# Windowed attention and a gated feed-forward in one kernel: the later attention blocks taken two at a time

## The chip, the core and the metric

The kernel runs on one core of one Trainium2 chip. The metric is the device time of one execution in microseconds (us). Before the change the median of three runs is 900.22 us (897.39, 900.22 and 904.76). The profiled execution of the same kernel took 901.14 us, of which 899.3 us lie between its first and its last instruction (the span).

## The reference

```python
scores = scale * q @ k.T                       # 8 batches, 8 heads, 576 positions, 64 wide
rel = pos[:, None] - pos[None, :]
mask_plain = (rel >= 0) & (rel < 32)                         # heads 0 to 3
mask_dil = (rel >= 0) & (rel < 128) & (rel % 4 == 0)         # heads 4 to 7
attn = softmax(where(mask, scores, -1e9))
x = (attn @ v), heads side by side             # 4608 rows of 512
h = x @ w_in                                   # 512 to 2048
g = h * clip(h + 3, 0, 6) / 6
out = g @ w_out                                # 2048 to 512
```

All of it is float32.

## The kernel before, in words

The **attention** is cut into 48 pieces `t`, called trios here. Since a query sees 32 keys at most (in the dilated heads too, once the host has sorted positions by their residue), a trio is 24 small problems: 32 queries against 64 keys. `block(ts, tv)` puts two trios on TensorE together: the scores of trio `ts` (`mm_scores`, L193, 24 products with a 64x32 weight) and, between them, the values of an earlier trio `tv` (`mm_values`, L211, 24 products). Each of these float32 products shows as two loads and two matmuls in the trace, so such a block is 96 loads and 96 matmuls. Its two results stand in two PSUM buffers.

Behind a block, for the scores: VectorE adds the mask (L222), takes the largest of each row (L226, `largest`) and subtracts it (L230, `shifted`), ScalarE takes the exponential (L239). The result `e` is turned by `turn_by_blocks`: two transposes on VectorE (L326, L327) and four DMAs of 24 KB on SyncE's queue (L330), which gives `a`, the weights of the value products. For the values: VectorE divides by the sums (L244, L245, L247, `normalise`), gives `x`, and the same `turn_by_blocks` makes `xf` of it. `st_split` then cuts `xf` in a high part `xh` (ScalarE, L358) and a low part `xl` (GpSimd, L363), the operands of the feed-forward. `shifted` also issues the load of a later trio's queries and keys (`kq`, 416 KB) and `normalise` that of a later trio's values (`v`, 390 KB), both on SyncE's queue; the pool `loads` has `NLOAD` = 3 buffers of each.

The **feed-forward** goes through 12 chunks of 384 rows and, for each chunk, 16 slices of the 2048 middle columns: one step `n` for each. A step is `gemm1(n)` on TensorE (12 matmuls of 384 columns, L458 to L460, into one of the two PSUM buffers of the pool `ps_h`), then `relu` on ScalarE (L466), `gate` on VectorE (L469, which sets the `ps_h` buffer free), `gate_high` on ScalarE (L473), `gate_low` on VectorE (L477), and two steps later `gemm2` on TensorE (9 matmuls of 512 columns, L490 to L492), which adds to three PSUM buffers of the pool `ps_a`. That pool has six buffers; three hold a chunk's sums, the others serve the attention. So a step is 21 matmuls and 21 weight loads. The tiles `e`, `a`, `x`, `xf`, `t`, `gh`, `gl` come from one pool `work` of `WORK` = 12 buffers.

The trios 0 to 11 and the first two chunks are worked off by a list written out by hand (`ORDER`). From trio 12 on, trios are set between the feed-forward steps by the table `at` near the end: `halves` counts half steps from the first step of chunk 2 (place 2s stands between `gemm1` and `gemm2` of step s, place 2s + 1 behind its `gemm2`). `st_both(t + 1, t)` at place `at[i]` makes one block (scores of trio t + 1, values of trio t) and its VectorE and ScalarE work; `xf` is turned one place later, `a` two places later, `st_split` four places later. There are 37 such blocks: the first with scores alone, 35 with both, the last with values alone. They stand 6 or 7 places apart at first and then 8, that is four steps. TensorE's order is the program's own; the other engines' order is made by a scheduler at build time, from priorities. A chunk's first `gemm1` waits for the `xl` of the last trio that has rows in it: in the steady part, one chunk in three has its last trio only six places ahead.

## Time and profile before

| what | before |
| --- | --- |
| median of three runs | 900.22 us |
| profiled execution | 901.14 us |
| its span | 899.3 us |
| TensorE matmuls (PE) | 884.3 us busy, 98% of the span, 8732 |
| TensorE weight loads (PEld) | 790.0 us busy, 8732 |
| VectorE (DVE) | 448.7 us busy, 50% |
| ScalarE (ACT) | 345.7 us busy, 38% |
| GpSimd (POOL) | 43.7 us busy, 5% |
| granted TensorE clock, mean | 0.99 |
| first changed block | at 176 us of the span |

PE in these rows is TensorE's matmuls, PEld its weight loads, which run beside them; SPq is SyncE's queue, on which most DMAs are issued. A matmul's duration is modelled and overlaps that of the next, so the distance from one start to the next says what one costs. "idle before <-" names what ended an engine's idle time; "issue" is idle time that ends with nothing that the profile shows. Where a group of rows has "waits", it is put down to the producer that came last.

### The profile page before, as it was taken

The numbers are of one execution on the slowest core, as the hardware profiler recorded it, in microseconds if no ns is written. First come the engines' busy times: TensorE is split into PE (matmuls) and PEld (weight loads), VectorE is DVE, ScalarE is ACT, GpSimd is POOL, SyncE is SP. The second block draws the span as 40 slices with busy tenths as digits, with TensorE's granted clock in tenths as the row PEclk, the third lists the DMA queues.
The fourth block names the chain that finished last, engine by engine and source line by source line (L and its number), as shares of the span: only waits on it lengthen the run. The fifth ranks groups of instructions, "written<-read, shape, count | busy, mean of one in ns | idle before, by whom it ended". The sixth has DMA issues, their size and how long they took to land.

```text
span 899.3 us, 20600 instructions
## 1 busy us (share of the span) xinstructions
PE 884.3 (98%) x8732; PEld 790.0 (88%) x8732; DVE 448.7 (50%) x951; ACT 345.7 (38%) x661; POOL 43.7 (5%) x60
## 2 busy tenths in 40 slices
PE   7899999999999999999999999999999999999998
PEld 4688898889898989998999899889988898899997
DVE  4799997245455545444444444454445444422221
ACT  3688775333333333323333333223333333322322
POOL 0000000000110100000010001000100000000000
PEclk8799999999999999999999999999999999999999
DMA  8746435122232213113212222122113210100000
GB/s 280 265 147 209 121 115 200 56 86 89 65 112 79 62 56 114 51 48 101 70 51 82 70 65 86 47 82 88 51 46 99 71 33 11 47 3 1 36 1 35
DMA packets 37803, 74.87 MB, mean 83 GB/s; under 512 B 7376, under 2 KB 16592, under 8 KB 37712
## 3 DMA queue, kind: packets, MB, share of 16 engines
q1 hardware_dynamic: 32528, 64.13, 23.3%
q10 hardware_dynamic: 5184, 9.44, 2.8%
q8 instruction: 68, 1.11, 0.5%
q14 instruction: 23, 0.19, 0.1%
HBM read 57.02 MB, written 9.44 MB: 74 GB/s over the span
## 4 chain that ended last, share of the span: by engine, by line
PE 95%; DVE 1%; ACT 1%; DMA 1%; SPq 1%; issue 1%; DVEq 0%; ACTq 0%
PE ps_o L490 15%; PE ps_h L458 15%; PE ps_h L460 14%; PE ps_h L459 14%; PE ps_o L492 14%; PE ps_o L491 14%; PE ps_a L211 3%; PE ps_a L193 2%; PE ps_a L203 1%; PE ps_a L296 1%; SPq L330 1%; DMA mi<-in_mask 0%; DMA a<-a_t 0%; PE ps_a L270 0%; DVE x L247 0%
## 5 line engine op out<-in xcount | busy, mean ns | idle before, releaser
L458 PE MATMUL ps_h<-xh,wt 128*128 128x384 f32 x768 | 261.0, 340 | 0.0
L469 DVE SCALAR_TENSOR_TENSOR t<-t,ps_h 128x384 f32<-128x384 f32 x192 | 106.3, 553 | 306.5 <-ACT t L466 306.2
L460 PE MATMUL ps_h<-xh,wt 128*128 128x384 f32 x768 | 258.7, 337 | 0.0
L459 PE MATMUL ps_h<-xl,wt 128*128 128x384 f32 x768 | 258.6, 337 | 0.0
L490 PE MATMUL ps_o<-wt,gh 128*128 128x512 f32 x576 | 228.2, 396 | 0.0
L492 PE MATMUL ps_o<-wt,gl 128*128 128x512 f32 x576 | 224.6, 390 | 0.0
L491 PE MATMUL ps_o<-wt,gh 128*128 128x512 f32 x576 | 224.2, 389 | 0.0
L466 ACT ACTIVATE t<-ps_h,three 128x384 f32<-128x384 f32 x192 | 111.0, 579 | 267.5 <-PE ps_h L460 260.0
L477 DVE TENSOR_TENSOR gl<-t,gh 128x384 fp32r<-128x384 f32 x192 | 107.1, 558 | 100.7 <-ACT gh L473 99.1
L458 PEld LDWEIGHTS ps_h<-xh,wt 128*128 128x128 f32 x768 | 144.9, 189 | 7.4
L459 PEld LDWEIGHTS ps_h<-xl,wt 128*128 128x128 f32 x768 | 144.8, 189 | 6.7
L460 PEld LDWEIGHTS ps_h<-xh,wt 128*128 128x128 f32 x768 | 144.8, 189 | 0.0
L473 ACT CAST gh<-t 128x384 fp32r<-128x384 f32 x192 | 98.4, 513 | 101.3 <-DVE t L469 96.7
L492 PEld LDWEIGHTS ps_o<-wt,gl 128*128 128x128 f32 x576 | 108.1, 188 | 23.4
L490 PEld LDWEIGHTS ps_o<-wt,gh 128*128 128x128 f32 x576 | 108.1, 188 | 18.7 <-issue 0.3
L491 PEld LDWEIGHTS ps_o<-wt,gh 128*128 128x128 f32 x576 | 108.2, 188 | 15.8
L363 POOL TENSOR_TENSOR xl<-xf,xh 128x384 fp32r<-128x384 f32 (+3 forms) x54 | 43.1, 808 | 740.6 <-ACT xh L358 675.4
L239 ACT ACTIVATE e<-e 128x384 f32<-128x384 f32 x48 | 25.1, 524 | 112.1 <-DVE e L230 112.1
L358 ACT CAST xh<-xf 128x384 fp32r<-128x384 f32 (+3 forms) x72 | 33.7, 536 | 37.0 <-DMA xf<-xf_t 36.8
L193 PE MATMUL ps_a<-kq 64*32 64x64 f32 x1872 | 46.6, 225 | 0.0
L211 PEld LDWEIGHTS ps_a<-v,a 64*32 64x32 f32 x1728 | 36.0, 105 | 10.7 <-issue 9.2
L211 PE MATMUL ps_a<-v,a 64*32 64x65 f32 x1728 | 42.4, 225 | 0.6 <-DMA a<-a_t 0.6
(46 smaller groups left out, 495.0 us busy)
## 6 DMA issues: line engine op xcount, KB each, us to landing
st<-in_w SPq DMA_DIRECT2D x32, 512.0 KB, 4.1
kq<-in_qk SPq DMA_DIRECT2D x39, 416.0 KB, 4.5
v<-in_v SPq DMA_DIRECT2D x39, 390.0 KB, 3.7
out<-o ACTq DMA_DIRECT2D x36, 256.0 KB, 2.9
first<-in_qk SPq DMA_DIRECT2D x9, 416.0 KB, 5.1
first<-in_v SPq DMA_DIRECT2D x9, 390.0 KB, 5.8
a<-a_t SPq DMA_DIRECT2D x144, 24.0 KB, 1.8
xf<-xf_t SPq DMA_DIRECT2D x144, 24.0 KB, 1.8
```

What stands on the lines that cost most here:

```text
L193: return nc.tensor.matmul(ps[at : at + QB, 2 * QB * i : 2 * QB * (i + 1)], lhsT=x[rows, KW + QB * n : KW + QB * (n + 1)], rhs=x[rows, QB * ...
L211: return nc.tensor.matmul(ps[at : at + QB, i * W : (i + 1) * W], lhsT=ats[t][rows, QB * n : QB * (n + 1)], rhs=vs[t][rows, n, :], start=Tr ...
L458: nc.tensor.matmul(ph, lhsT=wt[f][:, 0, ks], rhs=a, start=(kt == 0), stop=False)
L459: nc.tensor.matmul(ph, lhsT=wt[f][:, 0, ks], rhs=b, start=False, stop=False)
L460: ins = nc.tensor.matmul(ph, lhsT=wt[f][:, 1, ks], rhs=a, start=False, stop=(kt == NK - 1))
L466: return nc.scalar.activation(ts[n], phs[n], AF.Relu, bias=three, scale=1.0)
L469: return nc.vector.scalar_tensor_tensor(out=ts[n], in0=ts[n], scalar=6.0, in1=phs.pop(n), op0=ALU.min, op1=ALU.mult)
L473: return nc.scalar.copy(ghs[n], ts[n])
L477: return nc.vector.tensor_tensor(out=gls[n], in0=ts.pop(n), in1=ghs[n].bitcast(F32), op=ALU.subtract)
L490: nc.tensor.matmul(po[c][tt], lhsT=gh[:, rows], rhs=wt[f][:, 2], start=first, stop=False)
L491: nc.tensor.matmul(po[c][tt], lhsT=gh[:, rows], rhs=wt[f][:, 3], start=False, stop=False)
L492: ins = nc.tensor.matmul(po[c][tt], lhsT=gl[:, rows], rhs=wt[f][:, 2], start=False, stop=(f == NF - 1))
```

## The change

`st_both` becomes `st_pairs(ts, tv)`: two blocks directly behind each other, scores of ts and ts + 1 and values of tv and tv + 1. Four results need four PSUM buffers at once: the first block's scores stand in a buffer of the pool `ps_h` (the first product's), the other three in `ps_a`. The table `at` now holds one place for two trios: 1, 13, 25, 41, 57 and then every 16 places, eight steps; all of them are odd, behind a `gemm2`. Both `xf` are turned at the pair's own place, both `a` one place later, and `st_split` follows four and five places later. There are 19 such groups: one of two scores-only blocks, 17 pairs with both, one of two values-only blocks. `NLOAD` goes from 3 to 2 (so `ORDER` no longer loads `k14` and `v14`), `WORK` from 12 to 16. The lines behind `st_pairs` move by 10: L330 is now L340, L458 to L460 are L468 to L470, and so on.

```diff
-WORK = 12
+WORK = 16
-NLOAD = 3
+NLOAD = 2
...
-... k12 k13 k14 v12 v13 v14 M2 ...
+... k12 k13 v12 v13 M2 ...
...
-    def block(ts, tv):
+    def block(ts, tv, pool=ps_a, tag="ps_a"):
-        ps = ps_a.tile([P, 512], F32, name="ps_a") if ts is not None else None
+        ps = pool.tile([P, 512], F32, name="ps_a", tag=tag) if ts is not None else None
...
-    def st_both(ts, tv):
-        block(ts, tv)
-        if tv is not None:
-            normalise(tv)
-        if ts is not None:
-            largest(ts)
-            shifted(ts)
-            exponent(ts)
+    def st_pairs(ts, tv):
+        for i in range(2):
+            first = dict(pool=ps_h, tag="ps_h") if i == 0 else {}
+            block(ts and ts + i, tv and tv + i, **first)
+        if ts is not None:
+            largest(ts)
+        if tv is not None:
+            normalise(tv)
+        if ts is not None:
+            largest(ts + 1)
+        if tv is not None:
+            normalise(tv + 1)
+        if ts is not None:
+            for t in (ts, ts + 1):
+                shifted(t)
+                exponent(t)
...
-    at = [1 + 19 * i // 3 for i in range(10)]
-    at += [at[-1] + 8 * (i + 1) for i in range(T - NFIRST - 10)]
+    at = [1, 13, 25, 41, 57]
+    at += [at[-1] + 16 * (i + 1) for i in range((T - NFIRST) // 2 - len(at))]
-    place(-3, lambda: st_both(NFIRST, None))
-    place(-1, lambda: ats.update({NFIRST: turn_by_blocks(es.pop(NFIRST), "a")}))
+    place(-3, lambda: st_pairs(NFIRST, None))
+    place(-3, lambda: ats.update({t: turn_by_blocks(es.pop(t), "a") for t in (NFIRST, NFIRST + 1)}))
     for i, p in enumerate(at):
-        t = NFIRST + i
-        more = t + 1 < T
-        place(p, lambda t=t, more=more: st_both(t + 1 if more else None, t))
-        place(p + 1, lambda t=t: xfs.update({t: turn_by_blocks(xs.pop(t), "xf")}))
-        if more:
-            place(p + 2, lambda t=t: ats.update({t + 1: turn_by_blocks(es.pop(t + 1), "a")}))
-        place(p + 4, lambda t=t: st_split(t))
+        t = NFIRST + 2 * i
+        more = t + 2 < T
+        place(p, lambda t=t, more=more: st_pairs(t + 2 if more else None, t))
+        for j in range(2):
+            place(p, lambda t=t + j: xfs.update({t: turn_by_blocks(xs.pop(t), "xf")}))
+            if more:
+                place(p + 1, lambda t=t + 2 + j: ats.update({t: turn_by_blocks(es.pop(t), "a")}))
+            place(p + 4 + j, lambda t=t + j: st_split(t))
```

On TensorE, at the first changed place (behind the ninth matmul of a `gemm2`, at 176 us in the profile before), the program before has one scores-only block and then the next `gemm1`:

```order
L491 MATMUL ps_o<-wt,gh 128x512
L492 MATMUL ps_o<-wt,gl 128x512
L193 MATMUL ps_a<-kq 32x64 x24
L458 MATMUL ps_h<-xh,wt 128x384
L459 MATMUL ps_h<-xl,wt 128x384
```

The changed program has 48 products in one row there:

```order
L501 MATMUL ps_o<-wt,gh 128x512
L502 MATMUL ps_o<-wt,gl 128x512
L193 MATMUL ps_a<-kq 32x64 x48
L468 MATMUL ps_h<-xh,wt 128x384
L469 MATMUL ps_h<-xl,wt 128x384
```

The second block has moved up against the first, with no large matmul between them; at the later places 48 score and 48 value products follow each other in the same way.

On VectorE, in the steady part (z, mx and e belong to the block's sums, largest values and scores; t and gl to a feed-forward step), the program before has after a block eight operations, then the next step's gate:

```order
L244 TENSOR_SCALAR z<-ps_a 128x6
L245 RECIPROCAL z<-z 128x6
L247 TENSOR_TENSOR x<-ps_a,z 128x384
L222 TENSOR_TENSOR e<-ps_a,mi 128x384
L326 STREAM_TRANSPOSE xf_t<-x 128x192
L327 STREAM_TRANSPOSE xf<-x 128x384
L226 TENSOR_REDUCE mx<-e 128x6
L230 TENSOR_TENSOR e<-e,mx 128x384
L469 SCALAR_TENSOR_TENSOR t<-t,ps_h 128x384
```

The changed program has sixteen there, of which these are the last seven and what follows:

```order
L247 TENSOR_TENSOR x<-ps_a,z 128x384
L336 STREAM_TRANSPOSE xf_t<-x 128x192
L337 STREAM_TRANSPOSE xf<-x 128x384
L230 TENSOR_TENSOR e<-e,mx 128x384
L336 STREAM_TRANSPOSE xf_t<-x 128x192
L337 STREAM_TRANSPOSE xf<-x 128x384
L479 SCALAR_TENSOR_TENSOR t<-t,ps_h 128x384
L487 TENSOR_TENSOR gl<-t,gh 128x384
```

The gate of the step behind a pair has moved behind both blocks' work.

On SyncE's queue the program before issues, for each block, two loads and eight small DMAs:

```order
L173 DMA v<-in_v 128x780
L165 DMA kq<-in_qk 128x832
L330 DMA xf<-xf_t 32x192 x4
L330 DMA a<-a_t 32x192 x4
```

The changed program issues four loads ahead of the sixteen small DMAs of a pair:

```order
L173 DMA v<-in_v 128x780
L165 DMA kq<-in_qk 128x832
L173 DMA v<-in_v 128x780
L165 DMA kq<-in_qk 128x832
L340 DMA xf<-xf_t 32x192 x8
L340 DMA a<-a_t 32x192 x8
```

The small DMAs of a pair's first trio now stand behind two loads more, and those of its second trio behind the four of the first.

## The prediction, made before the changed kernel had run

> **What bounds the kernel now.** I read the page first: its span, its busy rows and the chain that ended last.

> ```profile
> span 899.3 us, 20600 instructions
> PE 884.3 (98%) x8732; PEld 790.0 (88%) x8732; DVE 448.7 (50%) x951; ACT 345.7 (38%) x661; POOL 43.7 (5%) x60
> ...
> q8 instruction: 68, 1.11, 0.5%
> ...
> PE 95%; DVE 1%; ACT 1%; DMA 1%; SPq 1%; issue 1%; DVEq 0%; ACTq 0%
> ```

> TensorE is the bound: 98% busy and 95% of the chain. So the change is worth what it does to the distances between TensorE's instructions, and all else counts only where TensorE comes to wait for it. Next I read TensorE's timeline round one steady block, the one behind the gemm1 that ends at 512.55.

> ```profile
> 512.38 0.34 PE L459 MATMUL ps_h<-xl,wt 128*128 128x384 f32 x1
> 512.55 0.34 PE L460 MATMUL ps_h<-xh,wt 128*128 128x384 f32 x1
> 512.82 0.24 PE L211 MATMUL ps_a<-v,a 64*32 64x65 f32 x1
> ...
> 513.06 0.30 PE L211 MATMUL ps_a<-v,a 64*32 64x65 f32 x3
> 513.15 0.24 PE L193 MATMUL ps_a<-kq 64*32 64x64 f32 x1
> ...
> 513.78 0.22 PE L193 MATMUL ps_a<-kq 64*32 64x64 f32 x1
> 513.93 0.50 PE L490 MATMUL ps_o<-wt,gh 128*128 128x512 f32 x1
> ```

> A large matmul of 384 columns takes 0.17 us (512.38 to 512.55). From 512.55 to the first small one it is 0.27, so going over costs 0.10. The 96 small ones start within 0.96 us, 10.1 ns apart in the mean, and going back costs 0.15. A block costs 513.93 - 512.55 - 0.17 = 1.21 us, of which 0.25 are the two changes of shape. The reader should also see the pace: some 35 small matmuls start in the first 0.25 us, then there is a break until 513.15, and the rest come 11 ns apart. TensorE's queue has instructions ready for the first stretch and is fed slower after that.

> The third view is what TensorE's loads waited for, above all the idle time that "issue" ends. In the hand-written early part, where small blocks follow each other closely, the timeline has the first five rows below; the sixth is the start of a block of the steady part, and the row of the waits that follows shows that the later blocks' loads (L211) had no such wait of over 0.4 us, the time of going over.

> ```profile
> 19.73 0.10 PEld L203 LDWEIGHTS ps_a<-first,a 64*32 64x32 f32 x1 [1.21 <-issue]
> 25.16 0.10 PEld L193 LDWEIGHTS ps_a<-first 64*32 64x32 f32 x1 [1.25 <-issue]
> 30.13 0.27 PEld L203 LDWEIGHTS ps_a<-first,a 64*32 64x32 f32 x15 [1.55 <-issue]
> 36.54 0.13 PEld L193 LDWEIGHTS ps_a<-first 64*32 64x32 f32 x1 [0.79 <-issue]
> 58.30 0.19 PEld L490 LDWEIGHTS ps_o<-wt,gh 128*128 128x128 f32 x1 [0.29 <-issue]
> ...
> 230.03 0.24 PE L211 MATMUL ps_a<-v,a 64*32 64x65 f32 x1
> ...
> PEld ps_a L211 <- issue: 9.2, 35, 0.4
> ...
> 19.72:25.15 5.43, 3.98 (x127) 2.88 (x126) 5.36 (x14) 4.39 (x10) 0.00 (x0) 1.00 0.88 314
> 25.15:30.12 4.97, 3.30 (x126) 2.64 (x127) 4.14 (x11) 3.92 (x9) 0.00 (x0) 1.00 0.79 241
> 30.12:36.53 6.41, 5.18 (x126) 3.47 (x126) 4.55 (x12) 3.16 (x7) 0.00 (x0) 0.63 0.98 328
> ```

> In the last three rows, stretches of time from one of these waits' end to the next, the first two counts are TensorE's matmuls and loads: 253, 253 and 252. With the three or four waits of its queue in each, that is 256 instructions, again and again. And the page's instruction queue moved 1.11 MB in 68 packets, 16.3 KB each, which for 17,464 instructions of TensorE is 64 bytes an instruction and 256 instructions a packet. So TensorE's code comes in blocks of 256, and these waits are waits for a block. Looking for such packets in narrow stretches (17.30 to 17.50, 55.80 to 56.20, 21.90 to 22.50, and 231.20 to 231.40 in the steady part), one finds one in each:

> ```profile
> q8 instruction: 1, 0.02, 33.7%
> q8 instruction: 1, 0.02, 15.0%
> q8 instruction: 1, 0.02, 17.9%
> q8 instruction: 1, 0.02, 39.8%
> ```

> The first two belong to the waits that end at 19.73 and 58.30: from a packet's start to the first instruction of its block pass 2.3 to 2.4 us, with the DMA engines full in the first case and nearly empty in the second. The third belongs to the wait that ends at 25.16, 3.2 us. The fourth starts 1.2 to 1.4 us after the small block that begins at 230.03. Counting instructions on from 19.73, a boundary lies 105 instructions into that block, that is at 230.03 + 0.53; the packet for the block behind it starts 0.6 to 0.8 us later. So one block ahead is fetched, upon entry into the block before it, and the instructions are there some 0.75 + 2.35 = 3.1 us after that entry. TensorE then waits only if it uses up 256 instructions sooner. Beside the large matmuls it can't:

> ```profile
> 19.72:176.10 156.38, 151.62 (x1529) 134.91 (x1528) 124.89 (x253) 105.14 (x205) 0.00 (x0) 0.97 0.51 163
> 800.00:825.00 25.00, 25.00 (x129) 22.84 (x128) 6.82 (x13) 6.75 (x13) 0.00 (x0) 1.00 0.00 1
> ```

> By the second row large matmuls and their loads go at 257 in 25 us. A block of small ones is 192 in 0.97 us, which leaves 64 large instructions, 6 us, before 256 are used. That is the cover which the change takes away.

> **The change part by part, on TensorE.** *Changes of shape.* 37 blocks become 19 groups, so 18 times a way back and a way over (0.25) is replaced by one more small step (0.01): 0.24 us. The second block may run at the slower pace throughout: 96 x 11 ns is 1.05 us and not 0.97, which leaves 0.15. I take 0.20: 18 x 0.20 = -3.6 us, between -2.7 and -4.3.

> *Waits for `a`.* In the steady part an `a` is made 16 us ahead of its use and will be 33 us ahead. Only two blocks, at 185 and 200 us, waited; these rows are the same for the stretch from 180 to 205 us:

> ```profile
> PE ps_a L211 <- DMA a<-a_t: 0.6, 2, 0.3
> ...
> PEld ps_a L211 <- DMA a<-a_t: 1.1, 3, 0.5
> ```

> That is up to 1.7 us. The second block now has 25 us and loses its wait. The first must have eight DMAs, one every 0.6 us, through SyncE's queue where four did; I estimate their last landing 0.3 us late. Sum -1.2 us, between 0 and -1.7.

> *Waits for code.* A pair is 384 small instructions in some 2 us. If a boundary lies early in it, the next one, 256 instructions or 128 matmuls x 10.1 ns = 1.3 us later, is reached before its code: 3.1 - 1.3 = 1.8 us of wait. I take 1.9, since some packets come later than that of the block at 230. A boundary in the first 50 instructions costs less, because TensorE's queue enters it that much ahead of its matmuls, at 10.3 instructions a us: none under 30. One beyond 150 costs nothing either: the next falls 22 or more large instructions behind the pair, 2 us. So about 100 of 256 positions are bad, and of 17 pairs some six or seven. They can be counted: from the boundary at 19.73 to 176.10 there are 1529 matmuls, 1528 loads and 25 waits of the queue, 3082 = 12 x 256 + 10. Going on with 42 instructions a step, 384 a pair and two or three waits, the boundaries lie at 224, 96, 226, 15, 60, 105, 150, 195, 240, 29, 74, 119, 164, 209, 254, 43 and 88 instructions into the 17 pairs (in the steady part each 45 further than the last, modulo 256). Bad are 96, 60, 105, 74, 119 and 88: 6 x 1.9 = 11.4; 43 costs some 1.2 and 150 some 0.1. Sum +12.7 us. The lower bound is 0, if code is fetched further ahead than I read; the upper one takes the longest way seen (3.2 and not 2.35) and all eight: 8 x 2.7 = 21.6.

> [...]

> **The change off TensorE.** In the profile before, a block's own work goes like this (VectorE, then ScalarE, SyncE's queue, GpSimd):

> ```profile
> 515.15 0.16 DVE L244 TENSOR_SCALAR z<-ps_a 128x6 f32<-128x6 f32 x1
> ...
> 515.57 0.56 DVE L247 TENSOR_TENSOR x<-ps_a,z 128x384 f32<-128x384 f32 x1
> 516.04 0.55 DVE L222 TENSOR_TENSOR e<-ps_a,mi 128x384 f32<-128x384 f32 x1
> 516.51 0.37 DVE L326 STREAM_TRANSPOSE xf_t<-x 128x192 f32<-128x192 f32 x1
> ...
> 517.26 0.51 DVE L226 TENSOR_REDUCE mx<-e 128x6 f32<-128x384 f32 x1
> 517.80 0.56 DVE L230 TENSOR_TENSOR e<-e,mx 128x384 f32<-128x384 f32 x1
> ...
> 521.12 0.89 ACT L358 CAST xh<-xf 128x192 fp32r<-128x192 f32 x2 [0.59 <-DMA xf<-xf_t]
> ...
> 517.40 2.41 SPq L330 DMA_DIRECT2D xf<-xf_t  x4
> ...
> 521.79 1.36 POOL L363 TENSOR_TENSOR xl<-xf,xh 128x192 fp32r<-128x192 f32 x2 [16.30 <-ACT xh L358]
> ```

> A block's eight operations take 3.2 us. With time from a pair's first small matmul, its first block ends at 1.2 and VectorE's sixteen at 1.25 + 6.4 = 7.7; the gate of the step behind the pair ends at 8.6. Its PSUM buffer is wanted by the gemm1 two steps on. A step is 4.1 us (21 of the 128.5 instructions of a kind that the row from 800 to 825 has in 25 us) and the first gemm1 begins at 2.1, so that is at 10.3: 1.7 us to spare. The borrowed `ps_h` buffer is free after the mask's addition, at 2 us, and wanted at 6.2. SyncE issues the first trio's four DMAs at 6.4 and the second's 2.4 us later; ScalarE has `xf` 3.7 us after such an issue (517.40 to 521.12), at 12.6, and GpSimd ends the second `xl` at 14.8. Where a chunk needs it, three steps behind the pair, its matmul comes at 2.1 + 3 x 4.1 + 7 x 0.17 = 15.6: 0.8 to spare. So I cost all of this at nothing; TensorE's own work hides it. The two load buffers are refilled 33 us ahead of their use, and the 16 work buffers replace waits that the trace doesn't have; both at nothing.

> **The sum**, against the profiled execution: 901.1 - 3.6 - 1.2 + 12.7 = 909.0. The median shown is 0.9 lower than that execution, so I forecast 908 us for the median, slower by 0.9%. A measurement of this kernel can tell about 1% from no change, so this is near that edge.

> **Rivals.** *The code is there in time.* Then only the first two terms count: 901.1 - 4.8 = 896.3, or 895.4 on the median's scale, faster by half a per cent. For it speaks that no block of the steady part waited; against it that none there used 256 instructions in under 7 us, while the early stretches, which used them in 4 to 6 us, did wait.

> *The clock falls in the waits.* Twice early on the granted clock was halved, one time after this stretch (the last three figures of a row are the clock, the DMA share and GB/s):

> ```profile
> 28.36:31.77 3.41, 1.47 (x46) 0.97 (x34) 2.79 (x8) 3.08 (x7) 0.00 (x0) 1.00 0.93 317
> 31.77:35.19 3.42, 3.29 (x101) 2.49 (x101) 2.30 (x4) 1.81 (x4) 0.00 (x0) 0.50 0.96 331
> ```

> TensorE was busy for 1.47 of 3.41 us. A wait of 1.9 us within one such stretch leaves about as much. At half speed for one stretch 1.7 us are lost: 908 + 7 x 1.7 = 920 if all seven waits do it, and it decides once three do (913). Against it: a stretch holds the whole of such a wait less than half the time, and the stretch from 19.72 to 25.15, with a wait of 1.25 us, kept the clock (1.00). [...]

> *The split comes late for the chunk.* Four loads instead of two ahead of the small DMAs, or a slower SyncE, put the second `xl` past 15.6. Two us late costs 1.2 at three chunks: 908 + 3.6 = 911.6. For it speaks the margin of 0.8 us; against it that in a pair that waits for code the chunk comes later too.

> **How the numbers follow.** The forecast's own case 55%; code in time 18%; clock 15%; late split 12%. The forecast's range is 903 to 914, from 1.3 to 2.7 us a wait. The stated range must reach down to the first rival: 895 to 914; what it leaves out is most of the clock's case and some of the rival's lower edge. Under 891, faster by over 1%: 3%, the first rival's tail. Over 909, slower by over 1%: 36% of the forecast's case (20%), the clock's case (15%), most of the late split (7%): 42%. Between: 55%.

> **What would show it.** In the changed profile TensorE's loads should wait for "issue" inside pairs, six or seven times, 1.5 to 2.2 us each, 256 instructions behind a boundary, in the pairs at places 13, 57, 73, 153, 169, (233) and 249, roughly 210, 312, 348, 528, 565, 708 and 745 us; a pair without such a wait should cost 2.2 us and not 2 x 1.21. The waits for `a` should be gone or under 0.5 us. The forecast is wrong if these waits are missing, if they are over 3 us, if the clock row shows stretches under 1.00 after 176 us, or if gemm1 waits for `xl` or for a gate.

## The result, and the profile after

| what | before | after |
| --- | --- | --- |
| median (7 runs each) | 899.16 us (897.17 to 904.76) | 908.35 us (906.66 to 909.53) |
| ratio of the two | | 1.0107, 95% interval 1.0087 to 1.0127 |
| profiled execution, its span | 901.14 us, 899.3 us | 906.66 us, 904.9 us |
| last large matmul ahead of the first changed block to the last matmul | 175.81 to 894.83: 719.0 us | 170.88 to 899.90: 729.0 us |

The changed kernel is slower by 1.1%. The two profiled executions differ less in span (5.6 us) than the part that was changed (10.0 us), since the hand-written early part, which the change leaves alone but for two loads and the numbers of buffers, took 4.9 us less in the execution after than in that before. That need not be an effect of the change: over the profiled executions of the changed kernel and of those below with the same buffers and no added products it ends at 170.9 to 176.7 us. The last row of the table is therefore the one to explain.

First the page of the changed kernel, at the places that were shown of before:

```profile
span 904.9 us, 20547 instructions
...
PE 880.6 (97%) x8732; PEld 793.0 (88%) x8732; DVE 445.4 (49%) x951; ACT 342.0 (38%) x661; POOL 44.7 (5%) x60
...
q8 instruction: 68, 1.11, 0.5%
...
PE 95%; DVE 2%; issue 1%; ACT 1%; DMA 0%; SPq 0%
```

The page says little: the same number of matmuls, slightly less of the span busy, and "issue" still at 1% of the chain. What TensorE waited for from 171 us on says more; the row that was shown of before (L211, 9.2 us in 35 waits, none over 0.4) is now this, with a second one beside it (us in total, times, longest):

```profile
PEld ps_a L211 <- issue: 10.9, 21, 2.1
PEld ps_a L193 <- issue: 8.9, 5, 2.3
```

Half as many ways over into small matmuls should have halved the first row. It grew instead, and single waits are over 2 us. The timeline of TensorE's loads shows the seven long ones, one pair each:

```profile
212.41 0.11 PEld L193 LDWEIGHTS ps_a<-kq 64*32 64x32 f32 x1 [2.27 <-issue]
313.55 0.10 PEld L211 LDWEIGHTS ps_a<-v,a 64*32 64x32 f32 x1 [2.13 <-issue]
352.87 0.10 PEld L193 LDWEIGHTS ps_a<-kq 64*32 64x32 f32 x1 [2.15 <-issue]
530.87 0.10 PEld L211 LDWEIGHTS ps_a<-v,a 64*32 64x32 f32 x1 [1.56 <-issue]
568.35 0.10 PEld L193 LDWEIGHTS ps_a<-kq 64*32 64x32 f32 x1 [1.95 <-issue]
710.08 0.10 PEld L211 LDWEIGHTS ps_a<-v,a 64*32 64x32 f32 x1 [0.83 <-issue]
747.89 0.10 PEld L193 LDWEIGHTS ps_a<-kq 64*32 64x32 f32 x1 [2.18 <-issue]
```

They are the pairs at places 13, 57, 73, 153, 169, 233 and 249, the seven that the count of instructions had named, and no other pair has one. Their sum is 13.1 us of TensorE's loads; between the small matmuls on both sides 13.5 us pass. A pair without such a wait looks like this on TensorE (the large matmul ahead, the first and the last small one, the large ones behind):

```profile
238.91 0.39 PE L502 MATMUL ps_o<-wt,gl 128*128 128x512 f32 x1
239.23 0.24 PE L211 MATMUL ps_a<-v,a 64*32 64x65 f32 x1
...
241.15 0.22 PE L193 MATMUL ps_a<-kq 64*32 64x64 f32 x1
241.30 0.44 PE L468 MATMUL ps_h<-xh,wt 128*128 128x384 f32 x1
241.58 0.34 PE L469 MATMUL ps_h<-xl,wt 128*128 128x384 f32 x1
241.75 0.34 PE L470 MATMUL ps_h<-xh,wt 128*128 128x384 f32 x1
```

From 238.91 to 241.30 less the large matmul's own 0.23 the pair costs 2.16 us, where two single blocks cost 2 x 1.21. The reader should also see the step behind it: from the first large matmul to the second it is 0.28 us, and only from there on 0.17. The same is in the profile before behind a single block:

```profile
513.93 0.50 PE L490 MATMUL ps_o<-wt,gh 128*128 128x512 f32 x1
514.26 0.40 PE L491 MATMUL ps_o<-wt,gh 128*128 128x512 f32 x1
514.50 0.40 PE L492 MATMUL ps_o<-wt,gl 128*128 128x512 f32 x1
```

There it is 0.33 and then 0.24. So each way back into large matmuls costs some 0.1 us more than the distance to the first of them shows, and a way that is saved is worth 0.24 + 0.11 = 0.35 us.

Last, the clock. Behind three of the seven waits, and nowhere else in the changed part, the granted clock (third figure from the end) is halved for one stretch. The stretches of 3.41 us round the first and the last of them:

```profile
209.05:212.47 3.42, 1.32 (x135) 1.15 (x122) 2.24 (x6) 0.52 (x1) 0.00 (x0) 1.00 0.53 130
212.47:215.88 3.41, 3.41 (x26) 3.24 (x27) 2.92 (x9) 0.00 (x0) 0.00 (x0) 0.50 0.81 227
...
744.95:748.36 3.41, 1.39 (x112) 1.13 (x98) 2.15 (x6) 0.52 (x1) 0.00 (x0) 1.00 0.40 124
748.36:751.78 3.42, 3.42 (x11) 3.42 (x12) 3.42 (x10) 0.00 (x0) 0.00 (x0) 0.50 0.45 124
```

In the stretches ahead of the three TensorE was busy for 1.32, 1.45 and 1.39 us. What a fall costs is read from pairs eight steps apart: with neither a wait nor a fall they start 35.3 us apart, behind the wait of 2.24 us at 743.9 it is 39.1, so 1.6 us go to the fall.

The account of the changed part: waits for code +13.5, falls of the clock 3 x 1.6 = +4.8, 18 changes of shape saved x 0.35 = -6.3, waits for `a` -1.3 (1.5 us in two single blocks before, 0.2 in the first pair now). That is +10.7; measured are +10.0, and the 0.7 between them is left open.

### The profile page after: what moved, and what is told of

Its sections match the earlier page's. It is cut to its first block, busy times and chain, and to the rows that moved or that the text cites. A ratio compares the mean times of both kernels' runs of the same rounds, so it can differ in the third digit from the quotient of the medians.

```text
span 904.9 us, 20547 instructions
## 1 busy us (share of the span) xinstructions
PE 880.6 (97%) x8732; PEld 793.0 (88%) x8732; DVE 445.4 (49%) x951; ACT 342.0 (38%) x661; POOL 44.7 (5%) x60
## 3 DMA queue, kind: packets, MB, share of 16 engines
q8 instruction: 68, 1.11, 0.5%
## 4 chain that ended last, share of the span: by engine, by line
PE 95%; DVE 2%; issue 1%; ACT 1%; DMA 0%; SPq 0%
PE ps_h L468 15%; PE ps_h L469 15%; PE ps_h L470 15%; PE ps_o L500 14%; PE ps_o L501 14%; PE ps_o L502 14%; PE ps_a L211 3%; PE ps_a L193 2%; PE ps_a L203 1%; PE ps_a L306 1%; DMA mi<-in_mask 0%; DVE x L247 0%; PE ps_a L270 0%; DVE e L230 0%; DVE mx L226 0%
## 5 line engine op out<-in xcount | busy, mean ns | idle before, releaser
L468 PE MATMUL ps_h<-xh,wt 128*128 128x384 f32 x768 | 263.4, 343 | 0.0
L470 PE MATMUL ps_h<-xh,wt 128*128 128x384 f32 x768 | 259.7, 338 | 0.0
L487 DVE TENSOR_TENSOR gl<-t,gh 128x384 fp32r<-128x384 f32 x192 | 112.8, 588 | 107.8 <-ACT gh L483 106.4
L468 PEld LDWEIGHTS ps_h<-xh,wt 128*128 128x128 f32 x768 | 145.6, 190 | 8.1 <-issue 0.2
L470 PEld LDWEIGHTS ps_h<-xh,wt 128*128 128x128 f32 x768 | 145.8, 190 | 0.0
L500 PEld LDWEIGHTS ps_o<-wt,gh 128*128 128x128 f32 x576 | 108.3, 188 | 15.6
L193 PE MATMUL ps_a<-kq 64*32 64x64 f32 x1872 | 43.6, 226 | 9.3 <-issue 9.3
L368 ACT CAST xh<-xf 128x384 fp32r<-128x384 f32 (+3 forms) x72 | 33.7, 535 | 47.6 <-DMA xf<-xf_t 47.4
L193 PEld LDWEIGHTS ps_a<-kq 64*32 64x32 f32 x1872 | 38.1, 105 | 8.9 <-issue 8.9
L211 PEld LDWEIGHTS ps_a<-v,a 64*32 64x32 f32 x1728 | 35.2, 105 | 11.0 <-issue 10.9
```

The lines of the kernel that those rows point to most:

```text
L193: return nc.tensor.matmul(ps[at : at + QB, 2 * QB * i : 2 * QB * (i + 1)], lhsT=x[rows, KW + QB * n : KW + QB * (n + 1)], rhs=x[rows, QB * ...
L211: return nc.tensor.matmul(ps[at : at + QB, i * W : (i + 1) * W], lhsT=ats[t][rows, QB * n : QB * (n + 1)], rhs=vs[t][rows, n, :], start=Tr ...
L468: nc.tensor.matmul(ph, lhsT=wt[f][:, 0, ks], rhs=a, start=(kt == 0), stop=False)
L470: ins = nc.tensor.matmul(ph, lhsT=wt[f][:, 1, ks], rhs=a, start=False, stop=(kt == NK - 1))
L487: return nc.vector.tensor_tensor(out=gls[n], in0=ts.pop(n), in1=ghs[n].bitcast(F32), op=ALU.subtract)
L500: nc.tensor.matmul(po[c][tt], lhsT=gh[:, rows], rhs=wt[f][:, 2], start=first, stop=False)
```

## The experiments

The theory: a pair loses 1.5 to 2.4 us when the boundary of a block of 256 instructions lies early in it, since the next block, entered 1.3 us later, is not there yet; merging as such is a gain. The first rival: pairs are slow for another reason (two loads more in SyncE's queue, the buffers, a burst on VectorE), and the count of instructions was lucky. The number in the text behind "offset" is the boundary's place in the pair, in instructions.

**The same pairs at other places.** Only the table of places differs; seven pairs are set a few half steps earlier or later, so that no offset lies between 41 and 126.

```diff
-    at = [1, 13, 25, 41, 57]
-    at += [at[-1] + 16 * (i + 1) for i in range((T - NFIRST) // 2 - len(at))]
+    at = [1, 17, 25, 41, 51, 77, 89, 105, 121, 137, 147, 165, 185, 201, 217, 235, 245, 265]
```

> The table alone is changed: the seven pairs that waited inside for code are moved by one to three steps (places 13 to 17, 57 to 51, 73 to 77, 153 to 147, 169 to 165, 233 to 235, 249 to 245), so that the boundaries of the 256-instruction blocks lie 12, 186, 21, 200, 203, 0 and 171 instructions into them; the work is the same. If the waits are for code: no wait inside a pair of over 0.3 us, none of the clock falls that stood behind three of them, so 13.4 us of waits and some 4.5 us of slow clock go: 908.35 - 17.9 = 890.5 us, 888 to 894, faster than before the change by about 1%. If the waits come of the pair itself (its four loads at once, the borrowed buffer, data that are late), they stay, wherever a pair stands: 905 to 912.

Measured: 891.55 us (890.42 to 892.68), 0.9915 of before (0.9895 to 0.9936). The waits of its changed part:

```profile
PEld ps_a L211 <- issue: 6.0, 17, 0.4
PEld ps_h L468 <- DVE t L479: 0.9, 1, 0.9
PEld ps_a L193 <- issue: 0.4, 1, 0.4
...
PEld ps_h L469 <- issue: 0.3, 1, 0.3
```

Inside the groups only the way over is left of "issue"; the last row is a short wait in the `gemm1` behind the pair at place 89. The clock stayed at 1.00. The changed part took 712.2 us, 6.8 less than before. So moving seven pairs by one to three steps, with the work, the loads and the buffers kept, turns 1.1% slower into 0.8% faster, and the rival has nothing left to explain. The wait of 0.9 us for a gate, at 717.5 us, is new: ScalarE stood 3.1 us until the DMAs of `xf` let it make `xh` at 715.58, and the `relu` behind that cast began at 716.25, though its `gemm1` had started its last matmul at 714.57. So a late split can cost TensorE time through ScalarE's order too, and not only through a late `xl`.

**Pairs at bad places.** The table again, now with 13 of the 17 offsets between 41 and 117.

```diff
+    at = [1, 13, 25, 37, 57, 73, 89, 99, 117, 135, 153, 169, 189, 201, 213, 233, 249, 265]
```

> The table alone is changed, the other way: six pairs that did not wait are moved (41 to 37, 105 to 99, 121 to 117, 137 to 135, 185 to 189, 217 to 213), so that the boundary lies 99, 64, 67, 70, 78 and 80 instructions into them. If the waits are for code: 12 full waits and the partial one, six more of 2.15 us, and some 2 or 3 more clock falls of 1.5 us: 908.35 + 12.9 + 3.9 = 925 us, 919 to 931. If the waits come of the pair itself, they don't follow the boundaries: 905 to 912.

Measured: 923.66 us (915.82 to 924.33), 1.0253 of before (1.0215 to 1.0292).

```profile
PEld ps_a L211 <- issue: 15.2, 22, 2.1
PEld ps_a L193 <- issue: 14.9, 9, 2.4
```

All 13 pairs with such an offset wait, 0.9 to 2.4 us each and 24.5 us together, and the four others don't. The clock fell three times. On the 712.2 us of the kernel without waits that makes 712.2 + 24.5 + 3 x 1.6 = 741.5 us for the changed part; it took 740.9. One of the four executions took 915.82 us, at a mean clock of 0.990 where the others have 0.980 to 0.985. It is not the one profiled, so that it had fewer falls is likely but not shown.

**More code ahead of the pairs.** The table is that of the changed kernel, but two steps ahead of the first pair 32 small products are added (128 instructions of TensorE, a result that nobody reads), so all offsets move by 128.

```diff
+    def more_code():
+        ps = ps_h.tile([P, 512], F32, name="more", tag="ps_h")
+        for i in range(32):
...
+    place(-7, more_code)
```

> The changed kernel with 32 small products more (128 instructions of TensorE) two steps ahead of the first pair, into a PSUM buffer that nobody reads; the table, the loads and all data are as in the change. If the waits are for code, they leave the seven pairs and turn up at places 1, 25, 105, 121, 201 and 217 (boundaries 96, 98, 67, 112, 81 and 126 instructions into the pair), about 2 us each, a shorter one perhaps at 41 (143) and 185 (36): nearly the same sum, 906 to 914 us with some 1.7 us for the added products. If the waits come of the pair itself, they stay at places 13, 57, 73, 153, 169 and 249.

Measured: 907.33 us (905.8 to 908.39), 1.0086 of before (1.0056 to 1.0117). TensorE's loads wait in six pairs:

```profile
188.49 0.10 PEld L193 LDWEIGHTS ps_a<-kq 64*32 64x32 f32 x1 [1.51 <-issue]
...
244.94 0.10 PEld L211 LDWEIGHTS ps_a<-v,a 64*32 64x32 f32 x1 [2.32 <-issue]
...
423.73 0.10 PEld L211 LDWEIGHTS ps_a<-v,a 64*32 64x32 f32 x1 [1.82 <-issue]
...
461.51 0.10 PEld L193 LDWEIGHTS ps_a<-kq 64*32 64x32 f32 x1 [2.29 <-issue]
...
641.72 0.10 PEld L193 LDWEIGHTS ps_a<-kq 64*32 64x32 f32 x1 [2.24 <-issue]
...
681.07 0.14 PEld L193 LDWEIGHTS ps_a<-kq 64*32 64x32 f32 x2 [2.19 <-issue]
```

They are the pairs at places 1, 25, 105, 121, 201 and 217, those that were named. The seven pairs that waited in the changed kernel, at the same places and beside the same work, don't. So it is not the place or the work at it; it is the count of instructions ahead.

Over these four kernels (68 pairs) the waits inside the pair, by the boundary's offset:

| offset | pairs | wait inside the pair |
| --- | --- | --- |
| 0 to 36 | 9 | none over 0.1 us |
| 41 and 43 | 2 | 1.0 and 0.9 us |
| 59 to 126 | 24 | 1.5 to 2.4 us |
| 143 to 254 | 33 | none over 0.2 us |

The last row is not quite free. The next boundary lies 256 instructions on, for an offset of 143 to 150 some 15 to 22 instructions behind the pair's 384, and there, in the `gemm1` that follows, TensorE waited behind three of the four pairs with such an offset (143, 149 and 150): 0.65, 0.75 and 0.29 us. The first of them is in the kernel with more code:

```profile
282.14 0.19 PEld L468 LDWEIGHTS ps_h<-xh,wt 128*128 128x128 f32 x1 [0.65 <-issue]
```

**The two blocks of a pair parted.** The first block of each pair stands one place earlier, between the step's `gemm1` and `gemm2`, so that nine large matmuls lie between the two; buffers, loads, table and the work off TensorE are those of the changed kernel.

```diff
-    def st_pairs(ts, tv):
-        for i in range(2):
-            first = dict(pool=ps_h, tag="ps_h") if i == 0 else {}
-            block(ts and ts + i, tv and tv + i, **first)
+    def st_first(ts, tv):
+        block(ts, tv, pool=ps_h, tag="ps_h")
+    def st_pairs(ts, tv):
+        block(ts and ts + 1, tv and tv + 1)
...
+        place(p - 1, lambda t=t, more=more: st_first(t + 2 if more else None, t))
```

> The changed kernel with the two blocks of a pair parted by the gemm2 of the step (one block ahead of it, one behind it); loads, buffers, the table and the work behind a pair are the same. If the loss is in 384 small instructions in a row: no wait for code inside a block, 37 changes of shape as before: 899.2 less 1.3 us of waits for the turned weights, 896 to 900 us. If the loss comes of the loads, the buffers or the table: 903 to 910.

Measured: 897.63 us (894.84 to 900.1), 0.9981 of before (0.9966 to 0.9997). The waits of its changed part:

```profile
PEld ps_a L211 <- issue: 11.0, 36, 0.4
PEld ps_a L193 <- issue: 0.6, 2, 0.4
```

None of the 38 waits is over 0.4 us: nine large matmuls, some 2 us, were cover enough for the next block in all of these groups. And against the shifted table, which has the same work and no waits for code inside its pairs either, this kernel has 19 changes of shape more: (897.63 - 891.55) / 19 = 0.32 us for each, a second measure of the 0.35 worked out from the rows. (It would be 0.37 if the shifted table's one gate wait of 0.9 us, which this kernel lacks, were taken out.)

**The buffers alone, and the pairs without them.** The kernel before with two load and 16 work buffers; and the shifted table with three and 12.

```diff
-WORK = 12
+WORK = 16
-NLOAD = 3
+NLOAD = 2
```

> The kernel before with the change's buffer edits alone (two load buffers, 16 work buffers, the two loads of trio 14 left out of the hand-written list), single blocks at the old places. My theory gives these edits nothing: 899.4 us, between 896 and 903, and no TensorE wait that the kernel before lacks. The rival, that part of the 9 us of the change is late loads from the two-buffer pool, would show here as 902 us or more, with waits of the small matmuls' loads for kq or v behind 176 us.

Measured: 899.09 us (896.04 to 901.31), 0.9997 of before (0.9982 to 1.0012). The edit costs and brings nothing by itself.

> The shifted table of pairs (no boundary of a code block at 41 to 126 instructions into a pair) with the buffers of before: 12 work buffers, three load buffers. A pair holds two e, two x, two xf and two a beside the t, gh and gl of three steps: if those 16 buffers were needed, relu or gate comes late and TensorE waits, 895 us or more, with PE rows waiting for ACT or DVE. If TensorE's 1.7 us of slack holds, it is as fast as the shifted table alone, 891.6 us, between 889 and 894. I think the first is likelier, at 893 to 900, since a pair's tiles live some 15 us.

Measured: 891.14 us (889.78 to 893.19), 0.9912 of before (0.989 to 0.9934). I had held the slower outcome likelier, and that was wrong: the pairs don't need the 16 buffers. One row came up that nobody had asked for:

```profile
487.30 0.10 PEld L211 LDWEIGHTS ps_a<-v,a 64*32 64x32 f32 x1 [1.81 <-issue]
```

With other buffers TensorE's program has 38 instructions less, waits of its queue that a change of buffers takes away. That moves the offset of the tenth pair from 29 to 49, and there the wait is. (A pair whose offset is 34 here waits 0.3 us, so the lower end of the table isn't sharp.) An edit that touches no matmul thus moved a wait of 1.8 us. Setting that pair one step later (offset 7) tests it:

```diff
-    at = [1, 17, 25, 41, 51, 77, 89, 105, 121, 137, 147, ...
+    at = [1, 17, 25, 41, 51, 77, 89, 105, 121, 139, 147, ...
```

> The shifted table with the buffers of before, and the tenth pair set at place 139 instead of 137, since there the boundary, 49 instructions into the pair, made a wait of 1.9 us; now it lies at 7. By the theory of the code blocks 891.1 - 1.9 = 889.2 us, between 887 and 892, with no wait for issue over 0.5 us in any pair. The rival, that the wait at that pair was the two trios' own data, leaves it at 891.1 us with a wait near 484 us.

Measured: 890.61 us (889.43 to 893.33), 0.9912 of before (0.9897 to 0.9928). The wait is gone, and no pair has one for "issue" over 0.4 us:

```profile
PEld ps_a L211 <- issue: 6.0, 17, 0.4
```

The changed part of the profiled execution took 711.1 us and not 713.6; the medians, 0.5 us apart with ranges that overlap, can't tell the two kernels apart. This is the fastest version here, beside the shifted table with the new buffers.

**All four results in one pool.** The shifted table, with the first block's scores in `ps_a` as well.

```diff
-            first = dict(pool=ps_h, tag="ps_h") if i == 0 else {}
+            first = {}
```

> The shifted table of pairs with all four results in the second product's pool (its six buffers, three of which hold the chunk's sums) instead of one in a buffer of the first product. Only three are then free, so the fourth result waits for the first block's mask addition, which ends some 2 us after the pair's first small matmul, and the second block starts some 0.9 us late: 17 pairs x 0.9 = 15 us, 907 us, between 899 and 912, with the small matmuls' waits put down to DVE. The rival: the order of the products hides it, 891.6 us, between 889 and 894.

Measured: 906.11 us (903.51 to 906.91), 1.0074 of before (1.0055 to 1.0093).

```profile
PE ps_a L193 <- DVE e L222: 11.0, 17, 0.8
```

Every one of the 17 pairs waits in its middle for VectorE's mask addition, and costs 0.9 us more (2.8 from its first to its last small matmul, and not 1.9). So the buffer of the first product is worth 14.6 us; without it the pairs are a loss even where the code is in time. The second block starts that much later, and none of these pairs waits for code besides.

**How much standstill halves the clock.** Since the falls were some 4.8 of the 10 us, I made waits of a chosen length in the kernel just told of, by having VectorE repeat the operation that the fourth result waits for (the results don't change). With the mask addition of a pair's first block done twice, three times and five times:

```diff
-            nc.vector.tensor_tensor(out=es[t], in0=ps[:, :CH], in1=mask_sb[:, 3 * kind + part], op=ALU.add)
+            for _ in range(1 + again):
+                nc.vector.tensor_tensor(out=es[t], in0=ps[:, :CH], in1=mask_sb[:, 3 * kind + part], op=ALU.add)
```

> The kernel with all four results in one pool, and VectorE's mask addition of a pair's first block done twice, so that TensorE's wait in each of the 17 pairs grows from 0.9 us by one addition, 0.56 us, to about 1.45 us. The theory of the clock (the granted clock is halved for one stretch of 3.41 us when TensorE stood still for more than 1.9 us of the stretch before) expects no fall after 60 us of the span and 906.1 + 17 x 0.56 = 915.6 us, between 913 and 919. A rival, by which each wait of 1 us or more has its chance of a fall, expects some falls and 920 us or more.

> The same with the addition done three times: waits of about 2.0 us. The wait alone gives 906.1 + 17 x 1.12 = 925.1 us. By the theory of 1.9 us in a stretch of 3.41 us a wait of 2.0 us gives a fall when it lies within one stretch, (3.41 - 2.0 + 0.2) / 3.41 = 0.47 of the time: some 8 falls of 17, each 1.7 us, 939 us, between 930 and 947. The rival, that only a stretch without any work makes the clock fall, expects none and 925 us (922 to 928).

> The same with the addition done five times: waits of about 3.1 us. The wait alone gives 906.1 + 17 x 2.24 = 944.2 us. By the theory a wait of 3.1 us fails to put 1.9 us into one stretch only when a stretch's end falls into the middle 0.7 us of it, so some 13 to 14 falls of 17, each 1.7 us: 967 us, between 958 and 973. The rival, that only a stretch without any work makes the clock fall, expects 944 us (941 to 949).

Measured: 915.51 us (914.89 to 916.21), 927.71 us (924.3 to 928.81) and 927.98 us (926.94 to 930.67). The first came out as expected, with no fall. The other two didn't. In both the standstill is 1.95 us in most pairs, 1.81 to 2.09 in all (this row is of the kernel with three additions, from 175 us on):

```profile
PE ps_a L193 <- issue: 27.9, 16, 1.9
```

The fourth result could also take the buffer that the first block's division sets free, and more additions don't delay that; the run with the division repeated, below, bears this out. So waits of 3.1 us were never made, and only two of the 34 waits had a fall behind them. Twelve of them put 1.9 us or more into one stretch, so a bound of 1.9 us is refuted. Standstill is counted here from the start of the last small matmul to that of the next, which is 0.2 us more than the idle time in these rows, since they count that matmul's modelled 0.22 us as busy. A stretch of the kernel with five additions, with 1.94 us of standstill and no fall behind it:

```profile
429.91:433.32 3.41, 1.67 (x148) 1.54 (x150) 2.55 (x8) 0.00 (x0) 0.00 (x0) 1.00 0.37 111
433.32:436.74 3.42, 3.42 (x76) 3.25 (x70) 3.32 (x9) 0.53 (x1) 0.00 (x0) 1.00 0.83 288
```

For longer waits the division is done twice too, between five additions:

> In the last two kernels the waits were 1.95 us in both, since the fourth result took the buffer that the first block's division (x) sets free, and more mask additions don't delay that one. Their 34 waits gave two falls of the clock, not some 20: a standstill of 1.9 us in a stretch is not enough as a rule. Over all runs so far a stretch with 2.09 us or more of standstill fell each time (6 of 6), one with 1.86 to 2.08 us in 4 of 16, one with less never. Here the division is done twice as well, between five mask additions, so that the wait should grow by one addition and one division to some 2.95 us: the wait alone makes 928 + 17 x 1.0 = 945 us. By the bound of 2.1 us a wait of 2.95 us gives a fall in (3.41 - 2.95 + 2 x 0.86) / 3.41 = 0.64 of the cases, 11 of 17, each 1.7 us: 964 us, between 956 and 971. The rival, that these falls belong to the waits for code and not to a standstill as such, or need a stretch without any work, expects 945 us (940 to 950) and at most two falls.

Measured: 954.54 us (954.45 to 956.81). The waits are 2.9 us, and the profiled execution has ten falls in 17, one of them here:

```profile
401.62:405.03 3.41, 0.74 (x70) 0.61 (x57) 3.08 (x8) 0.00 (x0) 0.00 (x0) 1.00 0.58 143
405.03:408.44 3.41, 3.41 (x79) 3.24 (x68) 3.33 (x9) 0.52 (x1) 0.00 (x0) 0.50 0.68 204
```

The time is below the 956 to 971 expected. That the waits are 2.88 and not 2.95 us, that a fall costs 1.4 to 1.6 us here and not 1.7, and that there is one fall less than counted makes some 5 of the 9 us; the rest is not explained. The falls as such came nearly as counted, ten for eleven. So they came with the standstill, whether the wait was for code or for VectorE. All falls of one execution begin on one grid of 3.41 us (in the changed kernel at 212.47, 314.87 and 748.36 us, 30 and 127 times 3.413 us apart), and by the standstill within one stretch of that grid the waits of all kernels here, from 100 us on, divide so (a wait that a stretch's end cuts in two gives two entries):

| standstill in the stretch | stretches | with a fall behind |
| --- | --- | --- |
| 1.0 to 1.86 us | 64 | 0 |
| 1.87 to 2.087 us | 18 | 5 |
| 2.091 to 2.88 us | 15 | 15 |

The line between the last two rows was drawn with the results known, between two entries that lie 4 ns apart; so it is no sharp bound.

## Why the prediction came out right, point by point

The forecast of 908 us lies on the measured 908.35. The mechanism was the one that was named, and the agreement of the numbers is in part luck, since two terms were off in opposite directions and the scale was off as well. One of the prediction's own signs of being wrong did come: three stretches behind 176 us have a clock of 0.50.

*Waits for code, +12.7.* Right in place, number and size: seven pairs, as counted, 13.5 us. The six bad ones took 1.65 to 2.32 us and not 1.9, offset 43 took 0.9 and not 1.2, offset 150 nothing. The condition at the other end, no wait under 30 and hardly any beyond 150, is what the table of offsets and the wait of 0.3 us at 34 show: inside the pair the ends lie at 34 to 41 and at 126 to 143, and up to 150 the `gemm1` behind waited up to 0.75 us. The rival that the code is there in time is refuted. With single blocks the crossing of a boundary cost nothing that shows (none of the 35 waits was over 0.4 us), in pairs at bad offsets it cost up to 2.4 us.

*Changes of shape, -3.6.* The step that failed in size. It took the way back as what lies ahead of the first large matmul, 0.15 us, and lowered the result for a slower pace of the second block. The second large matmul is late as well, by 0.11, and the second block's pace cost nothing that shows (2.16 us a pair, as 2 x 1.21 less 0.24 gives 2.18). So a merged change is worth 0.35 us by the rows and 0.32 by experiment, 18 x 0.35 = -6.3, outside the stated -2.7 to -4.3.

*Waits for `a`, -1.2.* Right: -1.3.

*The clock.* Given a chance of 15% as a case of its own, with all seven waits; in the profiled execution it came true in three, +4.8 us, which is where "it decides once three do" had it. It was wrong to treat it as a case that holds or not: each wait of 2 us has its chance, by where the grid lies, and the sum should have had the mean of it. Here the changes of shape made up for about half of it (+4.8 and -2.7).

*Off TensorE, 0.* Right: the buffers alone make 0.9997, no row of waits names `xl`, and the only one for a gate after 171 us is 0.2 us. The third rival, a late split, did not come about in the changed kernel.

*The scale.* The forecast was tied to the profiled execution before, 901.1 us. From the first changed block on the changed kernel is 10.0 us slower, where +7.9 was forecast. The medians are 9.2 us apart, where 908 less the 900.22 shown is 7.8; the median of before over seven runs is 899.16, 1.1 us lower, and so the two errors nearly cancel in the 908.

## What to carry to other kernels

## What the runs showed of the hardware that was not expected

- Kernels with the same work, data and buffers differ by 1.9% (891.55 and 908.35 us), and by 3.6% with the bad table (923.66), by where the boundaries of the code blocks fall.
- The wait for a block is not the same each time: 1.5 to 2.4 us at offsets from 59 to 126, without order in the offset (104: 2.4; 105: 2.2; 80: 1.7; 81: 2.3). Most of the difference goes with the packet that brings the block. From the packet's end to the block's first matmul pass 1.2 to 1.6 us in all 26 waits of the three kernels. Where the packet takes 1.2 us or more, the full waits are 2.1 to 2.4 us long; where it takes 1.0 us or less, they are 1.5 to 2.0 us, but for one of 2.2 us, whose packet began 1.3 us behind the boundary and not 0.6 to 1.0. The rows below are two such packets of the kernel with pairs at bad places, for the pairs at 99 (wait 2.4) and 189 (wait 1.5). The shares are those of 16 engines in 0.2 us (from 418.2 and from 627.5 us on), so the packets take 1.52 and 0.96 us. Why some take longer is open.

```profile
q8 instruction: 1, 0.02, 47.6%
q8 instruction: 1, 0.02, 30.1%
```

- The clock fell behind all 15 stretches of 3.41 us with 2.091 to 2.88 us of standstill, though TensorE worked in each of them, and behind five of the 18 with 1.87 to 2.087 us; what decides there the runs don't tell.
- The second large matmul behind small ones came 0.11 us late in the changed kernel (0.28 us behind the first at 241.30, where the next distance is 0.17) and 0.09 us late in the kernel before (0.33 at 513.93, where the next is 0.24).
